# An attention and expert-routing kernel with its written order of steps replaced by another

## Chip, cores and metric

The kernel runs on one core of a Trainium2 chip. The metric is the device time of one execution in microseconds; lower is better. Three runs of the kernel before were timed.

## What is computed

The inputs are q, k and v of 8 batches, 8 heads, 576 positions and 64 channels in float32, 4608 token ids, and the weights of 8 experts. Attention without a score matrix (softmax over channels for q, over positions for k) gives 4608 rows of 512; each row then goes through the one expert that its token id selects.

```python
q_s = softmax(q, axis=-1)
k_s = softmax(k, axis=2)
kv  = einsum('bhsd,bhse->bhde', k_s, v)
x   = einsum('bhsd,bhde->bhse', q_s, kv)      # as 4608 rows of 512
...
expert_idx = token_ids * 2654435761 % 8
for e in range(8):
    h = maximum(x[expert_idx == e] @ w1[e], 0)    # 512 -> 1024
    out[expert_idx == e] = h @ w2[e]              # 1024 -> 512
```

## The kernel before

First an index part sorts the tokens by expert on the chip: each expert has 640 slots, five blocks of 128. Then the work is cut into named steps. `_Steps` collects them, and the loop over `ORDER` at line 974 runs them one after the other; each step appends its instructions to the engines that it uses, so the order of the names is the order of every engine's instructions and of the transfers on POOL's queue (manual scheduling; the framework adds the waits). The names, with e an expert, b a batch and i or r a part:

- `K3`, `V3`: loads of k and v of a batch (L784, L788; k of batches 0 to 2 is loaded by SP, v of 0 and 1 by POOL, ahead of all steps). `EKb` is the exponential of k on ACT (L355, L356), `MKb` a copy of ones into v (L361), `KVb` the product k'v on PE, 20 matmuls (L373), `SCb` its scaling on DVE (L382 to L388).
- `Ge_i`: gather of 128 rows of q for block i of an expert (L396; O stands for the overflow rows). `EQ` is their exponential on ACT (L406), `SM` and `ML` sums and scaling on DVE (L416, L422), `TP` transposes on PE (L432), `TC` the copy out (L895, L887).
- `PPe_..`, `PCe_..`: x = q'(kv) on PE (L443 for experts 0 and 1, L455 after) and the copy out (L925, L931). `XP`, `XC`, `SH`, `SD`, `SI`, `SE` do the same for tokens beyond an expert's 72 per batch (L465 to L483).
- `We1_i`, `We2_i`: half i of the weights w1 or w2 of expert e (L508), into two sets of buffers, for even and odd experts, so that the weights of expert 3 wait until expert 1's layer is done. `Ae_lo_i`: matmuls of the first layer (L523); `R`: its relu (L536 on ACT, L538 on DVE); `Be_i`: second layer for one block, 8 matmuls (L545); `C`: copy out (L954 ACT, L956 DVE); `S`: scatter to the output (L550).
- `CNT`, `OVA`, `OHA`, `FND`, `FDD`, `QS`, `ROP`, `ROD`: overflow tokens. `ANY`: all engines read a flag and branch around a general path that these inputs don't need (L835, L836).

Half i of w1 holds 256 of the 512 rows of the matrix. A first-layer group accumulates four chunks of 128 rows for each 128 columns, the first two from half 0:

```python
for i in range(len(f)):
    for dc in range(DC):
        nc.tensor.matmul(p, lhsT=w1r[:, dc, f[i] * 128:(f[i] + 1) * 128], rhs=X[:, dc, :], start=(dc == 0), stop=(dc == DC - 1))
```

A name in the set `SWAP` sends that step's copy to the other of the two engines ACT and DVE (`other`, L486). A number behind a name, as in `KV2*9`, repeats so many matmuls of a constant before the step's own (L345, L346), into the bank that the step then overwrites. Between a load and a later transfer there is one more bond: a transfer from POOL reuses the semaphore of the eighth before it and waits for it.

Of the kernel before, what the change touches and what calls it, by code (L numbers as in the profile page):

```python
# [689 lines left out]
ORDER = """  # L690
ZO0 CNT MK0 OVA G0_2 OHA FND G0_1 G0_0 EK1 V2 ZO1 MK1 EQ0_0 G0_3 EK0 EQ0_2 EQ0_1 K3 EK2 FDD ANY V3 KV1 G0_4 SM0a G1_1
ML0a TP0_1 EQ0_3 EK3 KV0 GO_0 SC1 EQ0_4 EQ1_1 MK2 MK3 TC0_1 QS GO_1 SM0b K4 TP0_0 ROP G1_2 TC0_0 TP0_2 EQO_0 EQO_1
G1_0 SC0 K5 ML0b SMOa KV2*9 EQ1_0 GO_2 ROD GO_3 KV3 MLOa TC0_2 TP0_3 EQ1_2 TC0_3 EQO_2 TPO_0 TCO_0 G1_3 V4 SC3 SC2
SM1a TP0_4 EQ1_3 TC0_4 SM1b TPO_1*7 EQO_3 EK5 XP0*4 TCO_1 XP1 PP0_03 ML1a EK4 V5 MK5 PC0_03 XC0 PP0_02*4 XC1 K6 TP1_0
TC1_0 V6 ML1b K7 MK4 PC0_02 V7 TP1_1 W01_1 SH3 SH1 TC1_1 PP0_00 PP0_01 W01_0 EK6 G2_0 SMOb KV5 PC0_01 TP1_2 SD1 SH2
PC0_00 MLOb TP1_3 MK6 TC1_2 PP1_02 KV4 TC1_3 SD2 G3_1 PP1_03 PC1_02 TPO_3 EK7 SC5 MK7 SH0 SC4 TCO_3 G2_1 PC1_03 KV6
G2_2 TPO_2 SC6 TCO_2 PP0_41 SD3 KV7 SD0 PC0_41 PP0_43 PP0_42 SC7 XP2 PC0_42 PP0_40 PC0_43 PC0_40 PP1_01 XP3 PC1_01
PP0_61 XC2 G3_0 PP0_62 G3_2 PC0_61 PP1_43 XC3 PC0_62 W11_1 PP1_40 PC1_43 SI1 PC1_40 SI3 PP1_42 PP1_00 SE1 G3_3 PC1_42
PC1_00 A0_0_2 SI0 EQ3_1 SE3 PP0_63 A0_0_0 W11_0 PP0_60 G2_3 R0_0_2 SE0 W02_1 SI2 PC0_63 PP1_41 EQ3_0 R0_0_0 W02_0 G5_2
EQ2_1 G4_4 SM3a A0_0_1 R0_0_1 PC0_60 SE2 A0_0_3 PC1_41 ML3a R0_0_3 A0_576_0 EQ2_2 A0_432_0 A0_432_1 TP3_1 OV1 EQ2_0  # L700
R0_432_0 A1_0_0 R0_432_1 A1_320_3 G2_4 SM2a TP3_0 R1_0_0 ML2a TC3_1 EQ3_3 TC3_0 A1_0_3 TP2_1 R1_320_3 R1_0_3 TC2_1
W12_0 EQ3_2 A1_0_2 SM3b TP2_2 TC2_2 R0_576_0 TP2_0 A1_320_2 W12_1 EQ2_3 G6_2 G4_1 R1_320_2 ML3b B0_0 G5_3 TC2_0 B0_4
EQ2_4 C0_0 PP2_02 SM2b PC2_02 TP3_2 ML2b B0_1 TP3_3 A1_320_1 TC3_2 W21_0 G4_2 OV2 TP2_3 TC3_3 R1_0_2 TC2_3 TP2_4
A1_320_0 C0_4 C0_1 G7_2 G5_0 PP2_32 W21_1 R1_320_0 PC2_32 G4_3 TC2_4 B0_2 PP2_31 C0_2 PP2_03 PC2_31 PC2_03 A1_0_1
PP2_01 R1_0_1 B0_3 EQ5_3 S0_2 PP2_00 W31_0 OV4 PC2_00 R1_320_1 PC2_01 C0_3 B1_0 G5_1 PP2_33 G4_0 EQ5_2 EQ5_0 G7_3
W31_1 G6_3 PP2_30 PC2_33 S0_0 EQ4_3 B1_4 PC2_30 PP2_62 A2_0_1 A2_0_2 SM5b S0_3 PP2_63 PC2_63 C1_4 W22_1 ML5b C1_0
R2_0_2 EQ5_1 SM5a EQ4_2 B1_2 C1_2 R2_0_1 S0_1 A2_0_0 TP5_2 B1_1 A3_0_2 EQ4_4 OV3 R2_0_0 A3_0_3 TC5_2 PC2_62 EQ4_1
W22_0 R3_0_2 PP2_61 SM4b C1_1 PC2_61 ML5a G7_0 A3_0_1 ML4b R3_0_1 PP2_60 B1_3 PC2_60 TP4_4 EQ7_2 G6_0 C1_3 G6_1
A3_320_3 EQ4_0 R3_0_3 TC4_4 A2_0_3 R3_320_3 A2_320_2 R2_0_3 A2_320_3 R2_320_2 A2_320_1 R2_320_3 TP5_0 SM4a OV5 ML4a
W32_0 TP4_2 EQ7_0 R2_320_1 A2_320_0 R2_320_0 TC5_0 G7_1 S1_4 A3_320_1 G6_4 R3_320_1 W41_1 TC4_2 EQ6_2 S1_1 B2_2 TP4_0  # L710
PP4_61 EQ6_4 PC4_61 EQ6_1 EQ6_0 B2_4 A3_320_2 TC4_0 A3_0_0 C2_4 W41_0 EQ7_1 R3_320_2 W32_1 PP4_31 EQ7_3 SM6a B2_3
R3_0_0 PC4_31 C2_2 ML6a PP4_01 PP4_60 B2_1 C2_3 PC4_60 PC4_01 PP4_30 EQ6_3 A3_320_0 PC4_30 S2_3 B2_0 A4_320_3 W51_0
S2_4 W42_1 C2_1 SM7b R3_320_0 C2_0 ML7b S1_2 R4_320_3 SM7a A4_320_1 PP4_00 ML7a B3_1 R4_320_1 B3_0 A4_320_0 PC4_00
TP7_2 SM6b R4_320_0 ML6b S0_4 W51_1 A4_320_2 TP6_2 C3_0 R4_320_2 B3_2 S2_1 TC6_2 A4_0_3 C3_1 B3_3 TC7_2 C3_2 B3_4
R4_0_3 S3_0 A4_0_2 R4_0_2 C3_3 S3_3 A5_320_3 R5_320_3 A5_0_3 R5_0_3 W42_0 S2_0 A4_0_1 A5_320_1 TP6_4 R4_0_1 A5_320_0
R5_320_1 S1_0 TC6_4 R5_320_0 S2_2 OV6 W52_1 S1_3 A4_0_0 R4_0_0 TP6_0 S3_2 TP7_0 W52_0 C3_4 W61_0 A5_0_1 PP6_60 PC6_60
B4_1 A5_320_2 B4_4 TC7_0 C4_1 TC6_0 R5_0_1 S4_1 R5_320_2 C4_4 A5_0_0 R5_0_0 PP6_01 B4_0 C4_0 A5_0_2 R5_0_2 B4_3 PP6_00
PC6_01 PP6_31 PC6_00 PC6_31 B5_1 C4_3 S3_1 S3_4 C5_1 PP6_30 PP6_61 B4_2 PC6_30 C4_2 PC6_61 A6_0_2 A6_0_1 R6_0_1 B5_2
A6_320_1 R6_0_2 B5_3 W71_0 A6_0_0 S4_3 C5_3 B5_4 W62_0 OV7 R6_320_1 C5_4 A6_0_3 R6_0_0 R6_0_3 A6_320_0 C5_2 S4_2 B5_0
A7_0_2 S5_1 R6_320_0 A6_320_3 B6_0 R7_0_2 R6_320_3 S5_3 A6_320_2 S4_4 A7_320_0 C6_0 R6_320_2 S5_2 A7_320_2 R7_320_2  # L720
W72_0 B6_2 C5_0 S5_0 R7_320_0 A7_0_3 R7_0_3 C6_2 B6_1 A7_0_1 B6_3 R7_0_1 C6_1 S5_4 A7_320_3 C6_3 R7_320_3 A7_0_0 B6_4
C6_4 R7_0_0 B7_0 A7_320_1 C7_0 B7_1 S4_0 C7_1 R7_320_1 B7_3 B7_2 S6_2 S6_3 S6_0 C7_3 S6_4 S7_0 C7_2 B7_4a S6_1 S7_1
S7_3 S7_2 C7_4a B7_4b C7_4b S7_4
""".split()


# [299 lines left out]
```

## Time and profile before

| | |
|---|---|
| median of 3 runs | 222.04 us (221.56 to 222.4) |
| the profiled execution | 222.7 us, span of the trace 220.9 us |
| PE busy | 187.5 us, 85% of the span |
| DVE, ACT, POOL busy | 133.6, 113.7, 120.2 us |
| moved by DMA | 50.67 MB in 12904 packets |

Busy time is summed over the span, and an engine can be busy off the path that sets the end; the queues of transfers have a row of their own. A line of a timeline gives the start, the duration and in brackets the idle time before it with what ended it. Ends of matmuls are modelled and overlap the next start, so a matmul's pace is read from the distance of starts.

### The profile page before, as it was taken

The page shows a single profiled execution, that of the slowest core. Times are in us where ns is not written, and L with a number is a line of the kernel's source. Part 1 is how long each engine was busy: PE and PEld are TensorE (multiplying, and loading weights), DVE is VectorE, ACT ScalarE, POOL GpSimd, SP SyncE. Part 2 cuts the span into 40 slices and gives each one's busy share as a digit, 9 for nine tenths or more (in the row PEclk, how much of TensorE's full clock was granted, in tenths as well). Part 3 has the DMA queues.
Part 4 walks back from the last instruction along what each step waited for, and adds up shares of the span by engine and source line. Part 5 has one row for each costly group of instructions (what it writes and reads, how often), then busy time and mean ns, then how long its engine had stood idle before and what let it go on. Part 6 is the DMA issues. An engine that isn't in the chain of part 4 may idle for free.

```text
span 220.9 us, 3984 instructions
## 1 busy us (share of the span) xinstructions
PE 187.5 (85%) x1534; PEld 122.2 (55%) x1534; DVE 133.6 (60%) x260; ACT 113.7 (51%) x183; POOL 120.2 (54%) x152
## 2 busy tenths in 40 slices
PE   3501098669899999999899999999999999999990
...
PEclk9999999999999999999999999999999999999998
DMA  6999999999999999999996969938999996751342
GB/s 203 327 329 287 330 391 384 240 314 305 240 326 254 271 251 309 227 234 206 261 223 164 205 144 158 213 104 153 277 237 237 207 167 225 136 179 47 136 175 98
DMA packets 12904, 50.67 MB, mean 229 GB/s; under 512 B 2522, under 2 KB 2522, under 8 KB 11344
## 3 DMA queue, kind: packets, MB, share of 16 engines
...
q1 hardware_dynamic: 576, 3.71, 4.4%
...
## 4 chain that ended last, share of the span: by engine, by line
PE 51%; DVE 13%; issue 11%; POOL 6%; DMA 4%; POOLq 1%; ACT 1%; ACTq 0%
PE ph L523 24%; PE po L545 19%; POOL out_dram L550 6%; DMA w1r<-in_moe_w_dram 4%; DVE kvr L388 3%; PE t L432 3%; DVE rq L416 3%; DVE qs L422 2%; PE px L455 2%; PE t L443 1%; PE t L373 1%; PE t L472 1%; DVE XT L925 1%; DVE rec L384 1%; DVE XTov L478 1%
## 5 line engine op out<-in xcount | busy, mean ns | idle before, releaser
L523 PE MATMUL ph<-XT,w1r 128*128 128x320 f16 (+2 forms) x512 | 75.3, 297 | 1.3 <-DMA w1r<-in_moe_w_dram 1.3
L545 PE MATMUL po<-w2r,hT 128*128 128x512 f16 (+2 forms) x328 | 74.5, 374 | 0.0
L536 ACT ACTIVATE hT<-ph 128x640 f16<-128x640 f32 (+3 forms) x59 | 41.6, 709 | 57.6 <-PE ph L523 50.7
L550 POOL DMA_INDIRECT out_dram<-ob,sidx x40 | 41.6, 1041 | 51.7 <-DVE ob L956 32.5
L523 PEld LDWEIGHTS <-w1r 128*128 128x128 f16 x544 | 49.1, 98 | 23.0 <-DMA w1r<-in_moe_w_dram 1.6
L396 POOL DMA_INDIRECT raw<-in_q_dram,gidx x36 | 44.0, 1223 | 19.9 <-issue 6.9
L545 PEld LDWEIGHTS <-hT 128*128 128x128 f16 x328 | 31.2, 98 | 31.0
L956 DVE TENSOR_SCALAR ob<-po 128x512 f32<-128x512 f32 x32 | 21.6, 682 | 43.3 <-PE po L545 35.7
L416 DVE TENSOR_REDUCE rq<-qs 128x16 f32<-128x1024 f16 (+1 forms) x18 | 23.9, 1329 | 3.9 <-ACT qs L406 3.8
L406 ACT ACTIVATE qs<-raw 128x512 f16<-128x512 f32 x36 | 21.8, 630 | 7.3 <-DMA raw<-in_q_dram,gidx 5.5
L422 DVE TENSOR_TENSOR qs<-qs,rq 128x1024 f16<-128x1024 f16 (+1 forms) x18 | 24.0, 1337 | 0.2
L895 DVE COPY qT<-t 128x512 f16<-128x512 f16 (+1 forms) x19 | 9.9, 528 | 13.5 <-PE t L432 12.8
L432 PE MATMUL t<-ident,qs 128*128 128x128 f16 x160 | 13.7, 222 | 2.2 <-DVE qs L422 1.7
L432 PEld LDWEIGHTS <-qs 128*128 128x128 f16 x160 | 11.1, 100 | 4.5 <-ACT qT L895 1.8
L508 POOL DMA_DIRECT2D w1r<-in_moe_w_dram x14 | 8.2, 586 | 9.2 <-PE ph L523 6.7
L373 PE MATMUL t<-v,w1r 128*128 128x129 f16 x64 | 7.0, 266 | 5.3 <-ACTq L836 5.3
L508 POOL DMA_DIRECT2D w2r<-in_moe_w_dram x14 | 8.3, 595 | 5.5 <-PE po L545 3.0
L954 ACT ACTIVATE ob<-po 128x512 f32<-128x512 f32 (+2 forms) x9 | 4.9, 552 | 11.7 <-PE po L545 11.6
L925 ACT CAST XT<-t 128x288 f16<-128x288 f32 (+2 forms) x17 | 6.5, 400 | 7.8 <-PE t L443 7.7
L925 DVE CAST XT<-t 128x288 f16<-128x288 f32 (+2 forms) x15 | 6.5, 447 | 5.2 <-PE t L443 5.1
L931 ACT CAST XT<-px 128x864 f16<-128x864 f32 (+1 forms) x7 | 5.7, 810 | 6.7 <-PE px L455 6.7
L256 PE MATMUL po<-Z,AO 128*128 128x8 f16 x18 | 0.6, 175 | 9.9 <-DVE AO L244 9.9
(128 smaller groups left out, 197.5 us busy)
## 6 DMA issues: line engine op xcount, KB each, us to landing
...
```

The costliest lines, as they stand in the source:

```text
L396: nc.gpsimd.indirect_dma_start(out=raw[:, :], out_offset=None, in_=self.q[:, :], in_offset=bass.IndirectOffsetOnAxis(ap=idx[:, i:i + 1], a ...
L406: self.nc.scalar.activation(q16[:, i].rearrange("p h d -> p (h d)"), raws[i][:, :], ACT.Exp)
L416: nc.vector.reduce_sum(rv, qv, axis=AX.X)
L422: nc.vector.tensor_tensor(out=qf, in0=qf, in1=rv.rearrange("p i h -> p (i h)").unsqueeze(2) .to_broadcast([128, (hi - lo) * H_, DH_]), op= ...
L432: nc.tensor.transpose(pv[:, r, 128 * j:128 * j + 128], rq16[1][:, i + j, 2 * r:2 * r + 2, :] .rearrange("p h d -> p (h d)"), self.ident[:])
L508: self.nc.gpsimd.dma_start(w[what - 1][:, f], src[e, :, f])
L523: nc.tensor.matmul(p, lhsT=w1r[:, dc, f[i] * 128:(f[i] + 1) * 128], rhs=X[:, dc, :], start=(dc == 0), stop=(dc == DC - 1))
L536: self.nc.scalar.activation(to, fro, ACT.Relu)
L545: nc.tensor.matmul(po[:, 0:d.stop - d.start], lhsT=hT[:, fc, blk * 128:(blk + 1) * 128], rhs=w2r[:, fc, d], start=(fc == 0), stop=(fc == F ...
L550: sc = self.nc.gpsimd.indirect_dma_start(out=self.out[:, :], out_offset=bass.IndirectOffsetOnAxis(ap=self.ix.sidx[:, e, blk:blk + 1], axis=0),
L925: (A if other(f"PC{e}_{lo}{r}", r % 2 == 0) else V)(X[:, es, r, lo * CELL:hi * CELL], px[e, r, lo])
L956: nc.vector.tensor_scalar(out=obs[e, blk][:, d], in0=po[e, blk, x][:, 0:d.stop - d.start], scalar1=1.0 / SX, scalar2=None, op0=ALU.mult)
```

## The change

The tables `SWAP` and `ORDER` are replaced; no function is touched. The set of steps is the same, with the same transfers and buffers. In the new order W31_1 and W31_0, the two halves of expert 3's w1, follow each other on POOL's queue. The repeats go from 24 (KV2*9, TPO_1*7, XP0*4, PP0_02*4) to 30 (TP0_1*16, TP0_0*10, KV5*4). Cut to one line of each table:

```diff
 SWAP = set("""
-TC1_0 SD1 PC0_00 SD2 TCO_3 PC0_43 PC0_62 R0_0_3 TC2_0 C0_0 C0_2 R1_320_1 PC2_01 C0_3 PC2_30 PC2_63 PC2_61
...
+TCO_1 TCO_0 TC0_4 PC0_01 PC0_03 SD0 PC0_42 PC1_03 XC2 PC0_62 R0_0_2 C1_3 PC2_31 C1_4 C1_2 R3_0_0 TC4_2 C2_2
...
 ORDER = """
-ZO0 CNT MK0 OVA G0_2 OHA FND G0_1 G0_0 EK1 V2 ZO1 MK1 EQ0_0 G0_3 EK0 EQ0_2 EQ0_1 K3 EK2 FDD ANY V3 KV1 G0_4 SM0a G1_1
...
-PP2_01 R1_0_1 B0_3 EQ5_3 S0_2 PP2_00 W31_0 OV4 PC2_00 R1_320_1 PC2_01 C0_3 B1_0 G5_1 PP2_33 G4_0 EQ5_2 EQ5_0 G7_3
-W31_1 G6_3 PP2_30 PC2_33 S0_0 EQ4_3 B1_4 PC2_30 PP2_62 A2_0_1 A2_0_2 SM5b S0_3 PP2_63 PC2_63 C1_4 W22_1 ML5b C1_0
...
+G0_0 ZO0 G0_1 CNT G1_0 OVA OHA FND FDD ANY EK1 MK1 MK0 EK0 EQ0_1 KV1 K3 EQ0_0 ZO1 SC1 G0_2 EQ0_2 G1_1 V2 EK3
...
+PC2_01 EQ5_1 B0_1 G6_0 C0_0 C0_1 EQ5_2 PP2_00 PP2_03 PC2_00 B1_0 C1_0 W31_1 B1_3 C1_3 PP2_32 W31_0 SM5a B0_3
...
```

POOL's queue around expert 3's weights, before (w1r_1573 is expert 2's buffer, w1r_1679 expert 3's, w2r_1574 expert 2's second layer; raw are gathers, out_0_dram scatters):

```order
L508 DMA w1r_1573<-in_moe_w1_dram 128x2048
L396 DMA raw_1622<-in_q_dram,gidx_271 128x512
L550 DMA out_0_dram<-ob_1640,sidx_782 4608x512
L508 DMA w1r_1679<-in_moe_w1_dram 128x2048
L396 DMA raw_1697<-in_q_dram,gidx_271 128x512
L396 DMA raw_1705<-in_q_dram,gidx_271 128x512
L396 DMA raw_1711<-in_q_dram,gidx_271 128x512
L508 DMA w1r_1679<-in_moe_w1_dram 128x2048
L396 DMA raw_1716<-in_q_dram,gidx_271 128x512
L550 DMA out_0_dram<-ob_1527,sidx_782 4608x512
L550 DMA out_0_dram<-ob_1686,sidx_782 4608x512
L508 DMA w2r_1574<-in_moe_w2_dram 128x2048
```

And now (w1r_1615 is expert 2's buffer, w1r_1691 expert 3's, w2r_1616 expert 2's second layer):

```order
L508 DMA w1r_1615<-in_moe_w1_dram 128x2048
L550 DMA out_0_dram<-ob_1613,sidx_885 4608x512
L396 DMA raw_1662<-in_q_dram,gidx_271 128x512
L508 DMA w1r_1691<-in_moe_w1_dram 128x2048 x2
L550 DMA out_0_dram<-ob_1601,sidx_885 4608x512
L508 DMA w2r_1616<-in_moe_w2_dram 128x2048 x2
```

The three gathers between the halves are gone, one scatter and one gather stand ahead of both, and expert 2's second layer follows after one scatter.

ACT's queue at the start, before: the ones of v, the exponentials of k (kraw) and of q (raw), and the read of the flag with which the step ANY begins.

```order
L361 COPY v16_0_140<-two_95 128x20x2
L355 ACTIVATE w1r_299<-kraw1_138 128x2048
L356 ACTIVATE kt1_98<-kraw0_136 64x512
L361 COPY v16_1_142<-two_95 128x16x2
L406 ACTIVATE qs0_109<-raw_358 128x512
L355 ACTIVATE w1r_299<-kraw0_136 128x2048
L356 ACTIVATE kt0_97<-kraw0_136 64x512
L406 ACTIVATE qs0_109<-raw_329 128x512
L406 ACTIVATE qs0_109<-raw_354 128x512
L355 ACTIVATE w2r_300<-kraw2_144 128x2048
L356 ACTIVATE kt2_99<-kraw2_144 64x512
L835 TENSOR_LOAD flag_296
```

And now, first the flag, and from the end of the general path on, the first exponentials:

```order
L336 COPY kvr7_108<-zero_126 128x512
L837 TENSOR_LOAD flag_296
...
L355 ACTIVATE w1r_299<-kraw1_138 128x2048
L356 ACTIVATE kt1_98<-kraw0_136 64x512
L361 COPY v16_1_142<-two_95 128x16x2
L361 COPY v16_0_140<-two_95 128x20x2
L355 ACTIVATE w1r_299<-kraw0_136 128x2048
L356 ACTIVATE kt0_97<-kraw0_136 64x512
L406 ACTIVATE qs0_109<-raw_307 128x512
L406 ACTIVATE qs0_109<-raw_301 128x512
L406 ACTIVATE qs0_109<-raw_605 128x512
L355 ACTIVATE w2r_300<-kraw3_595 128x2048
```

The branch stands ahead of all exponentials now, the ones of v of batch 0 (v16_0) behind those of batch 1, and the k of batch 3 is taken before that of batch 2.

## Rows read from the trace of the kernel before

**Rows 1.** The page's part 2: the span in 40 slices, busy share in tenths.

```profile
PE   3501098669899999999899999999999999999990
...
PEclk9999999999999999999999999999999999999998
DMA  6999999999999999999996969938999996751342
```

**Rows 2.** Waits of PE over the whole span: total us, times, longest us.

```profile
PE ph L523 <- DMA w1r<-in_moe_w_dram: 1.3, 1, 1.3
```

**Rows 3.** Timeline of PE: start us, us, instructions, [idle before <-releaser].

```profile
62.33 1.63 PE L523 MATMUL ph<-XT,w1r 128*128 128x432 f16 x8
...
104.00 0.43 PE L523 MATMUL ph<-XT,w1r 128*128 128x320 f16 x2
105.70 2.08 PE L523 MATMUL ph<-XT,w1r 128*128 128x320 f16 x14 [1.26 <-DMA w1r<-in_moe_w_dram]
...
208.78 7.09 PE L545 MATMUL po<-w2r,hT 128*128 128x512 f16 x40
```

**Rows 4.** Timeline of POOL, which issues the transfers: same columns.

```profile
17.45 0.60 POOL L784 DMA_DIRECT2D kraw<-in_k_dram  x1
...
57.06 0.99 POOL L396 DMA_INDIRECT raw<-in_q_dram,gidx  x1 [1.47 <-DMA v<-in_v_dram]
...
62.41 1.02 POOL L396 DMA_INDIRECT raw<-in_q_dram,gidx  x1 [1.32 <-DMA w1r<-in_moe_w_dram]
...
91.30 0.62 POOL L508 DMA_DIRECT2D w1r<-in_moe_w_dram  x1
...
95.19 1.00 POOL L396 DMA_INDIRECT raw<-in_q_dram,gidx  x1 [0.61 <-ACT qs L406]
96.19 0.60 POOL L508 DMA_DIRECT2D w1r<-in_moe_w_dram  x1
...
215.13 0.98 POOL L550 DMA_INDIRECT out_dram<-ob,sidx  x1 [0.74 <-issue]
216.46 0.98 POOL L550 DMA_INDIRECT out_dram<-ob,sidx  x1 [0.35 <-issue]
```

**Rows 5.** The chain that ended last, around 96 us: start us, us, what.

```profile
96.19 9.46 DMA w1r<-in_moe_w_dram
```

**Rows 6.** Timeline of ACT, first steps and the last of the keys.

```profile
13.49 1.91 ACT L355 ACTIVATE w1r<-kraw 128x2048 f16<-128x2048 f32 x1
...
18.20 0.22 ACT L361 COPY v<-two 128x32 f16<-128x32 f16 x1 [2.15 <-DMA v<-in_v_dram]
20.66 0.63 ACT L406 ACTIVATE qs<-raw 128x512 f16<-128x512 f32 x1 [2.24 <-DMA raw<-in_q_dram,gidx]
...
54.35 1.91 ACT L355 ACTIVATE w2r<-kraw 128x2048 f16<-128x2048 f32 x1 [0.33 <-DMA kraw<-in_k_dram]
...
56.94 0.22 ACT L361 COPY v<-two 128x32 f16<-128x32 f16 x1
```

**Rows 7.** Lines 835 and 836, the branch on the routing flag, on SP.

```profile
L835 SPq TENSOR_LOAD <-flag x1: 457/457/457, 14.8 to 14.8; - x1
...
L836 SPq EVENT_SEMAPHORE  x8: 17/17/17, 16.2 to 18.7; - x8
```

**Rows 8.** Timeline of PE again: one form early and late, and the repeats.

```profile
27.56 0.64 PE L373 MATMUL t<-v,w1r 128*128 128x129 f16 x4
...
28.10 0.64 PE L373 MATMUL t<-v,w1r 128*128 128x129 f16 x4
...
33.14 2.17 PE L346 MATMUL t<-rowi,ident 128*128 128x512 f16 x9
...
39.82 0.61 PE L432 MATMUL t<-ident,qs 128*128 128x128 f16 x8 [1.66 <-DVE qs L422]
...
50.30 0.39 PE L373 MATMUL t<-v,w1r 128*128 128x129 f16 x4
...
50.58 0.39 PE L373 MATMUL t<-v,w1r 128*128 128x129 f16 x4
```

More of the change, by code (lines that the diff above doesn't have):

```diff
@@ L685 @@
 SWAP = set("""
-TC1_0 SD1 PC0_00 SD2 TCO_3 PC0_43 PC0_62 R0_0_3 TC2_0 C0_0 C0_2 R1_320_1 PC2_01 C0_3 PC2_30 PC2_63 PC2_61
-R2_320_1 C2_4 PC4_31 C2_0 C4_2 C6_4 R7_0_0 C7_4a C7_4b
+TCO_1 TCO_0 TC0_4 PC0_01 PC0_03 SD0 PC0_42 PC1_03 XC2 PC0_62 R0_0_2 C1_3 PC2_31 C1_4 C1_2 R3_0_0 TC4_2 C2_2
+TC4_4 R4_0_0 C5_4 R6_0_2 C7_4a C7_4b
 """.split())
 ORDER = """
-ZO0 CNT MK0 OVA G0_2 OHA FND G0_1 G0_0 EK1 V2 ZO1 MK1 EQ0_0 G0_3 EK0 EQ0_2 EQ0_1 K3 EK2 FDD ANY V3 KV1 G0_4 SM0a G1_1
-ML0a TP0_1 EQ0_3 EK3 KV0 GO_0 SC1 EQ0_4 EQ1_1 MK2 MK3 TC0_1 QS GO_1 SM0b K4 TP0_0 ROP G1_2 TC0_0 TP0_2 EQO_0 EQO_1
@@ L693 @@
[L693 to L702, printed above, removed]
```

52 lines of the change are left out of this document (33 added, 19 removed).

## Prediction

> **What bounds the kernel now.** I read the page's busy rows first. From the eleventh of the 40 slices TensorE shows 9 or more tenths to the last slice; before that it is mostly waiting, while the DMA row shows 9 from the second slice to the twentieth [rows 1]. So there are two stages, a front that feeds and a long stage that multiplies, and a time saved counts in the second stage only if TensorE stops idling there, or if that stage starts sooner.
>
> Where does the second stage start, and does it idle? The timeline of TensorE gives both. The first layer of expert 0 starts at 62.33 us and the last second-layer matmuls end at 208.78 + 7.09 = 215.87 us [rows 3]. In these 153.54 us the list of waits has one wait only, 1.26 us before a weight half of a first layer [rows 2, 3]. It stands after two matmuls of a step, and a first-layer step runs through half 0 of its weights for two matmuls before it needs half 1: the step is A3_0_2, the weights are expert 3's w1. So the stage is 152.28 us of matmuls and 1.26 us of idling, and
>
> end = start of A0 + 152.28 + idling + what follows the last matmul.
>
> What sets the start? POOL's timeline shows when a transfer has landed, since a transfer reuses the semaphore of the eighth before it. The last v load is down at 57.06 us and the second half of expert 0's w1 at 62.41 us [rows 4]. A0 starts at 62.33, as these weights land. ScalarE waits 0.33 us for the last k load at 54.35 us and marks the last v at 56.94 us, so the attention chain has almost no slack either [rows 6]. The front is bound by the DMA, with ScalarE close behind.
>
> And the stall? Half 0 of expert 3's w1 is issued at 91.30 us, half 1 only at 96.19 us: three query gathers stand between, the last of which waits 0.61 us for ScalarE to free its buffer [rows 4]. The chain that ended last runs through that second half: 9.46 us from issue to landing, at 105.65 us [rows 5].
>
> **The change, part by part.**
>
> *Expert 3's two halves side by side.* In the new order W31_1 and W31_0 follow each other with nothing between. Their gate is the same as before: expert 1's first layer must be through with the buffer, and the scatter and the gather ahead of them on POOL must be issued. If the first goes out at 91.30 as before, the second follows 0.62 us later, at 91.9. With the 9.46 us of the old second half it lands at 101.4. Expert 3's first step now also comes later on TensorE: one more second-layer block and one more first-layer group, 16 matmuls, stand ahead of it, and at 2.08/14 = 0.149 us each [rows 3] that is at least 2.4 us. So it comes near 107 us and its weights have about 5 us to spare. The stall goes: **-1.26 us**. Bounds: -1.26, and 0 if the halves are late for another reason. I take the lower end, because 5 us is more than all that moved. What is late next? Expert 2's second layer, whose halves are issued right behind expert 3's, and they are needed seven first-layer groups after A3 begins, 7 x 8 x 0.149 = 8.3 us; I see no wait there.
>
> *The start of A0.* The loads ahead of expert 0's w1 are the same transfers as before, all k, all v, the gathers of experts 0 and 1 and of the overflow rows, in another order. The DMA row is full all along, so the floor is no gain. It could be up to 0.4 us earlier, since W01_0 now goes first and two of the eight matmuls of A0's first row need only that half: 1.63 x 2/8 = 0.4 [rows 3]. What could make it later is the branch on the routing flag (the step ANY). ScalarE used to take it after the key exponentials EK1, EK0 and EK2; now it stands ahead of EK1. The flag is read at 14.8 us and the branch's semaphores are done from 16.2 us on [rows 7], so EK1, at 13.49 before, starts near 16.2, 2.7 us later. K3's load, now fourth on the queue, waits for EK1 to free its buffer: 16.2 + 1.91 = 18.1 us against 17.45 [rows 4, 6]. The queue is not empty then, as the gathers issued ahead of it are down only at 20.66 us [rows 6]. ScalarE itself waited 2.15 + 2.24 = 4.39 us for transfers before it got to EK0 [rows 6], which can swallow the 2.7. Later the exponentials for expert 0's fourth block stand behind two more gathers and both v loads, so some waits come back. Bounds for the start: -0.4, and +2.7 if nothing is absorbed. I take **+0.5**, near the lower end, because the row with 4.39 us of waits is the nearest to it.
>
> *Work after the start.* Steps moved across A0 cancel: before, SI0, SI2, PP0_63, PP0_60 and PP1_41 were still owed then, now SI1, SI0, PP1_43 and PP1_42. Both are 4 matmuls of 512 and 8 of 72 columns: 0.
>
> *The repeated matmuls* that keep TensorE busy in the front go from 24 to 30. At 2.17/9 = 0.24 us [rows 8] that is 1.4 us more, all ahead of A0 in the stage where TensorE waits; it is hidden while KV5, which carries four of them, is not the last thing ScalarE waits for. If that cover is gone, 4 x 0.24 = 1.0 us come on top.
>
> *Copies between VectorE and ScalarE* (the names swapped in the set): 24 names instead of 26. In the long stage both engines are far from full, so 0; in the front it is part of the +0.5.
>
> *The end.* The last scatter starts at 216.46, 0.59 us after the last matmul, because POOL is inside the scatter before it until 215.13 + 0.98 = 216.11 [rows 4]. The new order puts S7_3 earlier against the last block, so **-0.15**; bounds -0.35 (the last wait) and 0.
>
> Sum: -1.26 + 0.5 - 0.15 = -0.91 us. The profiled execution took 222.7 us, so 221.8; that execution lay 0.66 above the median of the three runs, 222.04, which makes **221.1 us** in the median.
>
> [...] The old repeats begin at 33.14 us with KV2 [rows 8] and go on with TPO_1, XP0 and PP0_02; the new ones come with TP0_1 and TP0_0, ahead of that, and then only with KV5, so that the stretch from KV2 to KV4, which waits much for VectorE, has none.
> [...]
>
> **The rivals.**
>
> *The front is bound by the DMA alone.* Then the start comes 0 to 0.4 us earlier, 0.2 in the middle: -1.26 - 0.2 - 0.15 = -1.6, **220.4 us**. For it: the full DMA row. Against it: ScalarE waits only 0.33 us for the last k load.
>
> *The stall stays or moves* to another weight half, as every order of 32 loads has a tightest one. Then +0.5 - 0.15 = +0.35, **222.4 us**. For it: the DMA row is full or nearly so to the middle of the span [rows 1]. Against it: the 5 us to spare.
>
> [...]
>
> **How the numbers follow.** A measurement of this kernel can tell about 0.5%, 1.1 us, from no change, so "faster" is below 220.9 and "slower" above 223.2. Chances: the forecast 0.48, whose spread of some 0.8 us puts 0.20 below 220.9 and 0.28 above; the DMA alone 0.19, 0.18 of it faster and 0.01 same; the stall elsewhere 0.13, same; the low level 0.20, of which 0.17 slower and 0.03 same. Faster 0.38, same 0.45, slower 0.17. The range reaches from the DMA rival less its 0.4 us of half-order and 0.2 us of end, 219.8, to the low-level rival, 223.3; outside lie half of that rival and some 0.08 below.
>
> **What would show it.** Right: no wait of TensorE for w1 after A0; the two halves of expert 3's w1 issued under 1.5 us apart and down before 104 us; A0 between 62.0 and 63.5 us; 152.3 us of matmuls from there to the end. Wrong: A0 later than 64 us, with ScalarE's last key exponential past 55.5 us; matmuls of KV4 or KV5 at 0.108 us; a new wait of TensorE for a weight half or for a copy after A0.

## The result and the profile after

The changed kernel took 224.96 us in the median of 4 runs (223.46 to 225.0), the kernel before 222.07 us on the same chip (221.56 to 222.4, 4 runs). The ratio is 1.0121 with a 95% interval of 1.0097 to 1.0146: slower by 2.7 us by this ratio, where 221.1 us and a range of 219.8 to 223.3 us were predicted. The execution profiled took 225.0 us, its span is 223.2 us (before 222.7 and 220.9). In this table the two profiled spans are taken apart:

| | before | after | difference |
|---|---|---|---|
| start of A0 | 62.33 | 66.35 | +4.02 |
| TensorE's wait for expert 3's w1 half | 1.26 | none | -1.26 |
| matmuls from A0 to the last | 152.28 | 152.04 | -0.24 |
| end of the last matmul to the end of the span | 5.03 | 4.81 | -0.22 |
| span | 220.9 | 223.2 | +2.30 |

So TensorE's wait, which the two halves side by side were to remove, is gone in this execution, -1.26 us as forecast, and the front gave back three times as much. The rows that answer to [rows 3], from the timeline of PE after (A0, expert 3's first step A3_0_3, and the last second-layer matmuls, which end at 209.57 + 8.82 = 218.39):

```profile
66.35 1.63 PE L523 MATMUL ph<-XT,w1r 128*128 128x432 f16 x8
...
110.57 1.25 PE L523 MATMUL ph<-XT,w1r 128*128 128x320 f16 x8
...
209.57 8.82 PE L545 MATMUL po<-w2r,hT 128*128 128x512 f16 x48
```

Expert 3's first step runs through its 8 matmuls in one row, without the break that stood at 105.70 before. It begins 44.22 us after A0, before 41.67. For [rows 4], the timeline of POOL after:

```profile
14.45 1.00 POOL L396 DMA_INDIRECT raw<-in_q_dram,gidx  x1 [0.31 <-issue]
18.14 0.58 POOL L786 DMA_DIRECT2D kraw<-in_k_dram  x1 [2.70 <-DVE at L235]
19.03 2.96 POOL L396 DMA_INDIRECT raw<-in_q_dram,gidx  x1 [0.31 <-issue]
...
46.30 0.53 POOL L790 DMA_DIRECT2D v<-in_v_dram  x1 [5.01 <-PE t L373]
...
63.13 1.00 POOL L396 DMA_INDIRECT raw<-in_q_dram,gidx  x1 [1.48 <-DMA w1r<-in_moe_w_dram]
...
94.66 1.17 POOL L508 DMA_DIRECT2D w1r<-in_moe_w_dram  x2
...
218.99 0.98 POOL L550 DMA_INDIRECT out_dram<-ob,sidx  x1 [0.30 <-ACT ob L956]
```

Both halves of expert 3 go out together at 94.66. But at 18.14 the load K3 is issued after 2.70 us in which POOL issues nothing, and V6, at 38.47 before, waits for KV2 until 46.30. Behind K3's late issue the DMA share falls to 0.79 and 0.83 for 4 us, where it is 1.04 and 1.03 before. In the table of stretches, the last three columns are TensorE's granted clock, the DMA engines' busy share and GB/s; first before, then after:

```profile
20.00:22.00 2.00, 0.65 (x18) 0.56 (x18) 1.89 (x3) 1.34 (x2) 1.99 (x1) 1.00 1.04 215
22.00:24.00 2.00, 0.00 (x0) 0.00 (x0) 0.86 (x8) 2.00 (x3) 1.41 (x2) 1.00 1.03 378
```

```profile
20.00:22.00 2.00, 0.65 (x18) 0.56 (x18) 1.24 (x3) 2.00 (x4) 1.99 (x1) 1.00 0.79 289
22.00:24.00 2.00, 0.32 (x4) 0.35 (x5) 1.12 (x7) 0.25 (x1) 1.70 (x3) 1.00 0.83 303
```

From 39 to 45.6 us, while V6 waits, the share is 1.02 again (row under e5).

For [rows 6], the timeline of ACT after:

```profile
15.94 1.91 ACT L355 ACTIVATE w1r<-kraw 128x2048 f16<-128x2048 f32 x1 [9.56 <-ACTq L838]
...
34.55 0.63 ACT L406 ACTIVATE qs<-raw 128x512 f16<-128x512 f32 x1 [5.41 <-DMA raw<-in_q_dram,gidx]
...
58.49 1.92 ACT L355 ACTIVATE w2r<-kraw 128x2048 f16<-128x2048 f32 x1
```

EK1 starts when the branch on the flag is done, 15.94, and ends at 17.85; K3, whose buffer it frees, is issued 0.29 us later. (The row of POOL names DVE at L235, which came last there; K3 needs nothing of it, since it goes out at 17.45 before, ahead of that instruction at 17.72.) ScalarE then waits 5.41 us for the gather of G0_3, which stands behind K3, two other gathers and two v loads, and the last key exponential EK7 starts at 58.49 instead of 54.35. The timeline of PE serves the repeats and the granted clock: the transposes of TP0_1 behind their 16 repeats, the wait in which the clock falls (1.00 from 36 to 39 us, 0.50 behind), KV2 and the first row of KV4; then the clock row of the page's part 2.

```profile
32.58 0.38 PE L432 MATMUL t<-ident,qs 128*128 128x128 f16 x4 [0.55 <-DVE qs L422]
...
39.61 0.61 PE L432 MATMUL t<-ident,qs 128*128 128x128 f16 x4 [2.07 <-DVE qs L422]
...
43.67 0.64 PE L373 MATMUL t<-v,w2r 128*128 128x129 f16 x4
...
44.21 0.64 PE L373 MATMUL t<-v,w2r 128*128 128x129 f16 x4
...
50.69 0.64 PE L373 MATMUL t<-v,w1r 128*128 128x129 f16 x4
```

```profile
PEclk9999999587999999999999999999999999999999
```

What the late start is made of stands in the chain of waits that ended last (start us, us, what), first of the change, then of the kernel before:

```profile
29.38 10.64 DMA rawo<-in_q_dram,oidx
...
43.87 2.14 PE t L373 x20
...
50.89 2.04 PE t L373 x20
52.93 0.86 PE t L346 x4
53.79 1.14 PE t L373 x20
```

```profile
31.85 1.14 DVE rq L416
...
34.80 1.22 DVE qs L422
...
46.30 0.86 PE t L346 x4
```

The chain of the change goes through the gather of the overflow rows, GO_0. It is issued at 29.38, before at 23.63, and ScalarE has its rows only at 40.02. KV2 and KV4 follow in the chain: KV2 runs at (44.21 - 43.67)/5 = 0.108 us per matmul and takes 2.14 us, KV4 2.04, and KV5, at (53.91 - 53.63)/5 = 0.056 us per matmul, 1.14. The granted clock is 0.50 from 39 to 45.6 us and 0.51 from 49.2 to 52.4, and 1.00 from 53 to 66: a stretch near 0.5, in which KV's matmuls come every 0.108 us, is called the low level here. The 1.9 us that KV2 and KV4 take longer than KV5 are the low level's part of this chain. The weights are not in it: the gather at 63.13 shows the first half of expert 0's w1 landed 3 us ahead of A0. The chain of the kernel before goes through VectorE's work from 29 to 60 us, but for 2 us of TensorE's around 46.30. So there were three suspects for the 4 us: the flag ahead of EK1 with K3 behind it, the low level, and the order on ScalarE and VectorE.

### The profile page after: what moved, and what is told of

Same layout as the page of the kernel before. It is cut to its first block, busy times and chain, and to the rows that moved or that the text cites. A ratio compares the mean times of both kernels' runs of the same rounds, so it can differ in the third digit from the quotient of the medians.

```text
span 223.2 us, 3990 instructions
## 1 busy us (share of the span) xinstructions
PE 192.2 (86%) x1540; PEld 125.9 (56%) x1540; DVE 135.4 (61%) x262; ACT 112.3 (50%) x181; POOL 117.8 (53%) x152
## 4 chain that ended last, share of the span: by engine, by line
PE 40%; issue 24%; POOL 11%; DMA 5%; ACT 4%; DVE 4%; POOLq 1%; ACTq 0%; DVEq 0%
PE ph L523 16%; PE po L545 14%; POOL out_dram L550 10%; DMA rawo<-in_q_dram,oidx 5%; PE t L373 4%; PE t L432 2%; PE t L443 1%; POOL w2r L508 1%; DVE kvr L388 1%; ACT qT L897 1%; PE t L472 1%; PE px L455 1%; ACT w2r L355 1%; DVE rq L416 1%; ACT qs L406 1%
## 5 line engine op out<-in xcount | busy, mean ns | idle before, releaser
L523 PE MATMUL ph<-XT,w1r 128*128 128x320 f16 (+2 forms) x512 | 73.8, 297 | 0.0
L396 POOL DMA_INDIRECT raw<-in_q_dram,gidx x36 | 39.8, 1104 | 20.9 <-issue 5.8
L958 DVE TENSOR_SCALAR ob<-po 128x512 f32<-128x512 f32 x34 | 23.3, 687 | 39.4 <-PE po L545 39.2
L432 PE MATMUL t<-ident,qs 128*128 128x128 f16 x160 | 14.4, 230 | 6.0 <-DVE qs L422 2.6
L897 DVE COPY qT<-t 128x512 f16<-128x512 f16 (+1 forms) x18 | 9.0, 511 | 10.7 <-PE t L432 10.5
L355 ACT ACTIVATE w1r<-kraw 128x2048 f16<-128x2048 f32 x4 | 7.6, 1909 | 9.6 <-ACTq L838 9.6
L933 DVE CAST XT<-px 128x864 f16<-128x864 f32 (+1 forms) x6 | 5.7, 953 | 7.8 <-PE px L455 7.8
L927 ACT CAST XT<-t 128x288 f16<-128x288 f32 (+2 forms) x18 | 7.4, 421 | 5.3 <-PE t L443 5.1
L373 PE MATMUL t<-v,w1r 128*128 128x129 f16 x64 | 7.9, 288 | 1.9 <-DVEq L838 1.9
L956 ACT ACTIVATE ob<-po 128x512 f32<-128x512 f32 (+2 forms) x7 | 3.7, 537 | 10.6 <-PE po L545 10.6
```

The costliest lines, as they stand in the source:

```text
L373: nc.tensor.matmul(pkv[:, r // 2, r % 2, 0:129], lhsT=k16t[:, f] if last else k16[:, c, f], rhs=v16s[e][:, c * NPAIR + r, 0:129] if last e ...
L396: nc.gpsimd.indirect_dma_start(out=raw[:, :], out_offset=None, in_=self.q[:, :], in_offset=bass.IndirectOffsetOnAxis(ap=idx[:, i:i + 1], a ...
L432: nc.tensor.transpose(pv[:, r, 128 * j:128 * j + 128], rq16[1][:, i + j, 2 * r:2 * r + 2, :] .rearrange("p h d -> p (h d)"), self.ident[:])
L958: nc.vector.tensor_scalar(out=obs[e, blk][:, d], in0=po[e, blk, x][:, 0:d.stop - d.start], scalar1=1.0 / SX, scalar2=None, op0=ALU.mult)
```

## The experiments

Each edit is a change of the written order of one of the two kernels, with all steps kept. Each run and the kernel before were timed on the same chip, but not all runs on one chip, so runs are compared by their ratios to the kernel before.

**e1: the halves alone.** In the kernel before, one name moved:

```diff
-W31_0 OV4 PC2_00 R1_320_1 PC2_01 C0_3 B1_0 G5_1 PP2_33 G4_0 EQ5_2 EQ5_0 G7_3 W31_1
+W31_0 W31_1 OV4 PC2_00 R1_320_1 PC2_01 C0_3 B1_0 G5_1 PP2_33 G4_0 EQ5_2 EQ5_0 G7_3
```

> The kernel before, with expert 3's second w1 half issued right behind its first and nothing else moved. If the new place of that half is what removed TensorE's 1.26 us of idling, the start of A0 stays at 62.3 us, no wait for w1r is left behind it, the span is 219.6 us (220.9 - 1.26) and the median near 220.8 us. If the stall only moves (to another weight half or to the gathers now issued later), the span is 220.5 to 221 us and the median near 222.

222.1 us (10 runs) against 221.94 (15 runs); ratio 1.0015, 0.9994 to 1.0035. In its profile the wait is gone, A0 starts at 62.70 and the span is 220.0, 0.9 under that of before. But in the median nothing is won. Either most executions have no such wait, or a shorter one, or they lose the time elsewhere; the profiled ones alone do not tell which.

**e8: the kernel before, profiled again.**

> The kernel before, unchanged, profiled once more on this chip. If the 1.26 us wait for expert 3's second w1 half belongs to every execution: the wait is 1.1 to 1.4 us again. If it varies with the arrival of transfers: under 0.8 us or none, in an execution whose span is under 220.5 us.

222.47 us, span 220.7, A0 at 62.66. The wait is there, with 0.77 us in place of 1.26:

```profile
105.46 2.08 PE L523 MATMUL ph<-XT,w1r 128*128 128x320 f16 x14 [0.77 <-DMA w1r<-in_moe_w_dram]
```

The span was not the short one that the expectation tied to a small wait. What varies is seen in the list of DMA issues around 96 us, where the last figure is the time from issue to landing: 9.46 us in the first execution of before [rows 5], here 9.0, and in e7 (below), whose queue is the same there, 7.8 and no wait. First e8, then e7:

```profile
w1r<-in_moe_w_dram POOLq DMA_DIRECT2D x1, 512.0 KB, 9.0
```

```profile
w1r<-in_moe_w_dram POOLq DMA_DIRECT2D x1, 512.0 KB, 7.8
```

**e2: the old front, the new order behind it.** Up to A0 the order of before, then the remaining steps of the change in their order; what the new front holds beyond the old one is put between:

```diff
 PP1_42 PP1_00 SE1 G3_3 PC1_42 PC1_00
+G2_4 PP0_63 W11_0 PP1_41 PC0_63 PC1_41 SE3 G4_2 SI2 PP0_60 EQ2_4 SE2
+A0_0_0 R0_0_0 EQ3_3 SI0 A0_0_3 G4_4 EQ3_2 PC0_60 R0_0_3
...
```

> Steps up to the first layer of expert 0 in the written order of before (with their choice of copy engine and their repeats), the remaining steps in the order of the change. If all of the loss lies in the front: A0 at 62.3 us, no wait for w1r after it, 152.0 us of matmuls, span 219.6 us, median near 220.8 us. If part of the loss lies behind the start of A0 (copies, scatters), span above 220.5 us with A0 at 62.3 us.

228.21 us, ratio 1.0296 (1.0245 to 1.0346), A0 at 63.88. It doesn't tell the front of the change from its rest, since the joint makes a wait of its own: EQ2_4 follows its gather at once and stands ahead of the first relu on ScalarE (timeline of ACT), and TensorE waits for that relu (timeline of PE).

```profile
69.26 0.63 ACT L406 ACTIVATE qs<-raw 128x512 f16<-128x512 f32 x1 [6.06 <-DMA raw<-in_q_dram,gidx]
69.80 0.87 ACT L536 ACTIVATE hT<-ph 128x864 f16<-128x864 f32 x1
```

```profile
70.72 1.62 PE L523 MATMUL ph<-XT,w1r 128*128 128x432 f16 x8 [3.33 <-ACT hT L536]
```

In this run one gather with its use right behind it cost TensorE these 3.33 us.

**e3: the flag back.** In the changed kernel:

```diff
-FDD ANY EK1 MK1 MK0 EK0 EQ0_1 KV1 K3 EQ0_0
+FDD EK1 MK1 MK0 EK0 EQ0_1 K3 ANY KV1 EQ0_0
```

> The changed kernel, with the branch on the routing flag put back behind EK1, EK0, EQ0_1 and the issue of K3 (and KV1 behind it), nothing else. If the flag's delay of EK1 (15.94 us instead of 13.49) and with it of K3's load makes the late start: EK1 back near 13.5 us, A0 1.5 to 2.5 us earlier than 66.35, median 222.5 to 223.5 us. If the delay is swallowed by ScalarE's later waits for transfers (5.41 us before EQ0_3), A0 stays within 0.5 us of 66.35 and the median near 225.

223.75 us (6 runs), ratio 1.0062 (1.0023 to 1.0101); EK1 at 12.81, K3 issued at 15.46 right behind the gathers, ScalarE's wait before EQ0_3 2.56 us instead of 5.41, A0 at 63.68, 2.67 earlier. So the flag matters, but by which way? ScalarE's first exponentials of q came no earlier than in the change, at 21.05 against 21.12, which points to the transfers. By the ratios 1.3 us come back, with intervals that just overlap.

**e6: K3 behind two gathers, the flag kept first.** In the changed kernel:

```diff
-KV1 K3 EQ0_0 ZO1 SC1 G0_2 EQ0_2 G1_1 V2
+KV1 EQ0_0 ZO1 SC1 G0_2 EQ0_2 G1_1 K3 V2
```

> The changed kernel with the flag's branch kept first, but the load K3 (whose buffer comes free only when EK1 is done) issued behind the gathers G0_2 and G1_1 instead of ahead of them. If the flag costs its time through POOL's queue, with K3 blocking what is issued behind it while the DMA queues run dry at 20 to 24 us: POOL's 2.70 us of idling ahead of K3 goes, the DMA share is 1.0 from 20 to 24 us, the gather for EQ0_3 lands at 31 to 32.5 us instead of 34.55, A0 is 1.5 to 2.5 us earlier, median 222.5 to 223.7 us. If it costs it through ScalarE, whose exponential EK1 starts at 15.94: A0 stays within 0.5 us of 66.35, median near 225.

222.46 us (10 runs), ratio 1.0024 (1.0004 to 1.0044) where the change has 1.0121: one load moved by two places on POOL's queue takes back 2.2 us, and the intervals lie apart. EK1 still starts at 15.95. POOL's timeline has no idle time ahead of K3 any more. Of the 2.70 us, 1.24 remain ahead of the gather at 16.69, where the branch stands in POOL's order; the rest was the wait for EK1. The DMA engines are full from 20 us (same columns as above):

```profile
16.69 0.99 POOL L396 DMA_INDIRECT raw<-in_q_dram,gidx  x1 [1.24 <-DVE m L227]
17.99 1.00 POOL L396 DMA_INDIRECT raw<-in_q_dram,gidx  x1 [0.31 <-issue]
18.99 0.59 POOL L784 DMA_DIRECT2D kraw<-in_k_dram  x1
```

```profile
20.00:22.00 2.00, 0.65 (x18) 0.56 (x18) 1.25 (x2) 2.00 (x4) 1.70 (x3) 1.00 1.04 361
22.00:24.00 2.00, 0.37 (x4) 0.40 (x5) 1.11 (x7) 0.97 (x2) 1.39 (x3) 1.00 1.03 378
```

The gather of EQ0_3 is there at 31.72, and GO_0 is issued at 25.59 instead of 29.38. One thing moves along with it: KV2 now runs at 0.056 us per matmul, the granted clock is 0.51 from 48 to 50 us, 0.64 from 50 to 52 and 1.00 in the rest from 36 to 56, so up to 1.0 of the 2.2 us can be the clock's (20 matmuls, 2.14 us in the change and 1.15 here). The execution profiled, 223.93 us, is the longest of the ten, and its A0 at 65.29 is only 1.06 earlier; why, its chain of waits shows (start us, us, what):

```profile
30.14 5.61 PE t L346 x16
35.75 0.22 PE t L432 x4
35.97 2.16 PE t L346 x10
```

The repeats stand in the chain: TP0_1, whose input VectorE has scaled at 32.3, waits behind its 16 until 35.75, and TP0_0 behind 10 more.

**e7: the flag first in the old order.** In the kernel before:

```diff
-FND G0_1 G0_0 EK1 V2 ZO1 MK1 EQ0_0 G0_3 EK0 EQ0_2 EQ0_1 K3 EK2 FDD ANY V3
+FND G0_1 G0_0 FDD ANY EK1 V2 ZO1 MK1 EQ0_0 G0_3 EK0 EQ0_2 EQ0_1 K3 EK2 V3
```

> The kernel before, with only the branch on the routing flag (and the vector step FDD) put ahead of EK1. EK1 starts near 15.9 us. By the theory of the blocked queue K3 stands behind V2 and G0_3 here, POOL loses under 1 us, ScalarE swallows the rest in its 4.39 us of waits for transfers: A0 at 62.3 to 63.2 us, median 222 to 222.8. If the delay of EK1 itself runs down ScalarE's chain: A0 at 64.3 to 65 us, median 224 to 224.8.

221.32 us (10 runs, 221.14 to 221.77) against 222.17 (19 runs, 221.32 to 222.97); ratio 0.9967, 0.9951 to 0.9982. EK1 is as late as in the change, and the kernel is faster than before. V2 and G0_3 go out ahead of K3 while EK1 runs:

```profile
16.42 0.58 POOL L788 DMA_DIRECT2D v<-in_v_dram  x1 [0.96 <-DVE mine L220]
17.31 1.03 POOL L396 DMA_INDIRECT raw<-in_q_dram,gidx  x1 [0.31 <-issue]
18.34 0.59 POOL L784 DMA_DIRECT2D kraw<-in_k_dram  x1
```

**e9: K3 at the head in the old order.** The order of e7 with K3 moved:

```diff
-FDD ANY EK1 V2 ZO1 MK1 EQ0_0 G0_3 EK0 EQ0_2 EQ0_1 K3 EK2
+FDD ANY EK1 K3 V2 ZO1 MK1 EQ0_0 G0_3 EK0 EQ0_2 EQ0_1 EK2
```

> The kernel before with the flag's branch ahead of EK1, as in the run named e7 (221.32 us), and in addition the load K3 issued first behind the branch, ahead of V2 and G0_3. By the theory of the blocked queue this puts the loss of the change into the old order: POOL idles about 2.7 us ahead of K3 (issue at 18.1 us), the DMA share falls under 0.9 from 20 to 24 us, and the kernel loses 1.5 to 2.5 us against e7: A0 at 64 to 65.2 us, median 222.8 to 223.8 us. If K3's place does not matter by itself (the change lost its time to its orders on ScalarE or VectorE): A0 within 0.4 us of e7's 62.70, median 221.2 to 221.7.

223.01 us (10 runs), ratio 1.002 (0.9996 to 1.0044): 1.2 us more than e7 by the ratios (1.69 by the medians, on two chips), and the intervals lie apart. POOL idles as in the change, GO_0 is issued at 25.42 instead of 23.68, A0 is at 65.25; the DMA share in 20 to 22 us is 0.91 and 1.07 in the next 2 us, so the queue hardly ran dry, against 0.79 and 0.83 in the change. The price is that of the order: what stands behind K3 goes out later.

```profile
18.01 0.58 POOL L784 DMA_DIRECT2D kraw<-in_k_dram  x1 [2.71 <-DVE at L235]
18.58 0.59 POOL L788 DMA_DIRECT2D v<-in_v_dram  x1
```

The execution profiled, 224.22 us, is the longest of the ten, and its granted clock is 0.66 over 40 to 50 us. But the loss does not need the low level: the four executions of e9 with a mean granted clock of 1.0 took 222.49 to 223.17 us, and none of the ten of e7 more than 221.77. With e6 this is the same cause taken out of one order and put into the other: 2.2 and 1.2 us.

**e4 and e12: the repeats exchanged.** e4 is the changed kernel with the repeats of before, e12 the kernel before with those of the change:

```diff
-TP0_1*16 ... TP0_0*10 ... KV5*4
+KV2*9 ... TPO_1*7 ... XP0*4 ... PP0_02*4
```

> The changed kernel, with the repeated matmuls taken from TP0_1, TP0_0 and KV5 and put where they stood before (9 with KV2, 7 with TPO_1, 4 with XP0, 4 with PP0_02), all else as in the change. If the low level of TensorE's clock from 39 to 52 us makes the late start: matmuls of KV2 and KV4 at 0.056 us, POOL's issue of V6 some 1 to 2 us before 46.3, A0 at 63.5 to 65 us, median 222 to 223.7 us. If the feeding of the front alone sets the start, the low level goes and A0 stays within 0.5 us of 66.35, median near 225.

> The kernel before with the repeats of the change: 16 with TP0_1, 10 with TP0_0 and 4 with KV5, none with KV2, TPO_1, XP0 and PP0_02. If the place of the repeats is a cause of its own: low granted clock somewhere from 39 to 53 us, KV2 or KV4 at 0.108 us, A0 0.5 to 1.5 us later, median 222.7 to 223.7. If they are covered in this order: A0 within 0.3 us of 62.5, median 221.8 to 222.4.

Both lose: e4 227.29 us, ratio 1.0214 (1.0161 to 1.0267); e12 227.41 us, ratio 1.0177 (1.0103 to 1.0251). In e4 no repeats stand ahead of KV2, the granted clock is 0.62 in 30 to 40 us and 0.70 in 40 to 50, and KV2's 9 repeats take 3.70 us in the timeline, where 2.17 was the price before [rows 8]; 3.50 of them stand in its chain of waits:

```profile
42.96 3.50 PE t L346 x9
```

In e12 the 16 repeats stand in front of TP0_1, which ran at 29.18 in the kernel before, and ScalarE waits for the transposes behind the repeats (timelines of PE, where the first of the 16 lies ahead of this row, and ACT); the low level comes later (granted clock 0.63 in 44 to 46 us, 0.50 from 46 to 54):

```profile
29.76 3.95 PE L346 MATMUL t<-rowi,ident 128*128 128x512 f16 x15
33.55 0.39 PE L432 MATMUL t<-ident,qs 128*128 128x128 f16 x4
```

```profile
37.49 0.58 ACT L895 COPY qT<-t 128x512 f16<-128x512 f16 x1 [2.93 <-PE t L432]
```

**e5: more repeats.** The changed kernel with 22 more, in the gaps that TensorE has from 37.6 to 49.2 us:

```diff
-TP0_3 ... TP0_2 ... TPO_1 ... TPO_0 ... XP0
+TP0_3*8 ... TP0_2*6 ... TPO_1*2 ... TPO_0*4 ... XP0*2
```

> The changed kernel with its 30 repeats kept and 22 more put where TensorE idles between 37.6 and 49.2 us: 8 with TP0_3, 6 with TP0_2, 2 with TPO_1, 4 with TPO_0, 2 with XP0. If the low level of TensorE's clock is a cause: granted clock 1.00 from 39 to 53 us, KV2 and KV4 at 0.056 us, V6 issued 1 to 2 us before 46.3, A0 between 64.3 and 65.5 us, median 223 to 224 us. If the clock only follows from the late feeding and is covered by other waits: the clock rises, A0 stays within 0.4 us of 66.35, median near 225. If the repeats stand in the way of ready work: A0 later than 66.8.

225.12 us, ratio 1.0169 (1.0107 to 1.023): no gain in the median. Its four executions took 223.69, 224.81, 225.42 and 227.23 us at mean granted clocks of 1.0, 0.996, 0.987 and 0.981. The first is the one profiled, and the shortest: the clock stays at 1.00 and A0 comes at 65.02, 1.33 earlier than in the change. Stretches of the change, then of e5 (PEclk is the third last figure):

```profile
39.00:45.60 6.60, 3.99 (x34) 3.61 (x35) 5.79 (x13) 5.79 (x9) 1.62 (x3) 0.50 1.02 249
49.20:52.40 3.20, 3.20 (x32) 3.20 (x33) 3.07 (x5) 2.98 (x8) 2.10 (x2) 0.51 1.02 281
```

```profile
39.00:45.60 6.60, 4.20 (x45) 2.89 (x44) 5.73 (x14) 5.80 (x9) 1.91 (x5) 1.00 1.02 247
49.20:52.40 3.20, 3.20 (x51) 2.73 (x49) 3.03 (x7) 2.94 (x8) 1.52 (x2) 1.00 1.03 253
```

So this one execution without the low level starts A0 1.33 us earlier. In the other three, whose mean clock is lower, that is gone; they have no profile that shows where.

**e11, e13, e14, e15: what is left in e6.** One edit on top of e6 each, but for e14 (on e13) and e15 (on e14):

```diff
 e11
-V3 ... G0_3 G0_4
+G0_3 G0_4 V3
 e13
-TP0_1*16 ... TP0_0*10
+TP0_1*6 ... TP0_0
 e14
-TPO_1 ... TPO_0
+TPO_1*5 ... TPO_0*4
 e15
-SC1 ... SM0a QS
+SM0a QS SC1
```

> The run named e6 (222.46 us) with the load V3 issued behind the gathers G0_3 and G0_4 as well, so that the two v loads, which move some 205 GB/s from 24 to 28 us, no longer stand together ahead of the gathers. If the order of these loads is what is left of the loss: ScalarE's wait of 2.48 us ahead of EQ0_3 shrinks to under 1.2 us, A0 0.5 to 1.2 us earlier than e6's 65.29, median 221.3 to 222.0. If the rest lies in ScalarE's and VectorE's order: the wait only moves behind (rawo), A0 within 0.3 us, median 222.2 to 222.7.

> The run named e6 (K3 behind the gathers, 222.46 us) with 6 repeats instead of 16 with TP0_1 and none instead of 10 with TP0_0; the 4 with KV5 stay. In e6's profile TP0_1 stands behind its 16 repeats until 35.58 us, while its input is ready at 32.4, and TP0_0 behind 10 more. If the repeats have become the bound there, once the loads come earlier: TP0_1 at 32.5 to 33.5 us, A0 1 to 2.5 us earlier than e6's 65.29, median 220.8 to 221.8 us. If they are needed to hold the clock: granted clock 0.5 in more of 30 to 53 us than e6's 48 to 51, median 222.5 to 225. If the work behind waits for loads anyway: median 222.2 to 222.7.

> The run named e13 with 5 repeats with TPO_1 and 4 with TPO_0 besides, where TensorE idled 1.55 and 1.26 us in e6. If the clock's fall at 48 us costs KV4 its 20 x 0.052 = 1.0 us and these repeats prevent it: KV4 at 0.056 us, 0.5 to 1 us faster than e13. If the clock does not fall in e13 or the repeats stand in the way: no gain, or up to 1 us slower than e13.

> The run named e14 (222.25 us) with VectorE's step SC1 behind SM0a and QS instead of ahead of SM0a. In e14 VectorE idles until 25.99 us for SC1's matmuls (KV1), then works without a gap from 27.4 to 45 us, and the chain runs through it. SM0a's input is there at about 25.5 us. If VectorE's late start is the rest of the loss: SM0a at 25.5 to 26 us, VectorE's row 0.5 to 1.4 us earlier, A0 at 62.8 to 63.7 us instead of 64.17, median 221.2 to 221.8. If ScalarE or the transfers are as late on their own: A0 within 0.3 us of 64.17, median 222.0 to 222.5.

e11 takes 223.49 us, ratio 1.006 (1.0024 to 1.0096), a loss against e6: the waits for the gathers go, and ScalarE waits 3.21 us at 32.92 for V3 instead (the execution profiled, 222.89 us, has A0 at 63.61, but the ten reach 225.2). e13: 222.43, ratio 1.0008 (0.9988 to 1.0028); TP0_1 now runs at 32.45, but the granted clock is 0.50 to 0.51 from 38 to 50 us, and KV2 and KV4 run at 0.108 (the execution profiled, 223.56 us, is the longest of the ten). e14: 222.25, ratio 1.0021 (1.0005 to 1.0036); the granted clock is 0.67 in 44 to 46 us and 1.00 from 46 to 56, KV4 runs at 0.056. e15: 222.22, ratio 1.0003 (0.9973 to 1.0032); VectorE's first sum starts at 24.40 instead of 27.36, and the chain then runs through a transfer, the overflow gather. These three can't be told from e6: in their profiles, where one chain is cut, another of nearly the same length sets the start (A0 at 64.81, 64.17 and 64.26 us, in e6 at 65.29). e13 also says something of the low level: the executions of the change had mean granted clocks of 0.974 to 0.984 and took 223.46 to 225.0 us; the seven of e13 within the same clocks took 221.78 to 222.63.

**e10: e7 with the halves.** The move of e1 on top of e7.

> The run named e7 with expert 3's second w1 half issued right behind the first as well. If what hid the gain of the halves was only the spread of the front's end, e7's narrower spread (221.14 to 221.77 us) shows it: 0.3 to 0.8 us less than 221.32. If e7 has no such wait left in most executions (its profile shows none): median 221.2 to 221.5 us, no difference.

221.65 us (10 runs, 221.24 to 223.8), ratio 0.9983 (0.9946 to 1.002): no gain over e7. e7 is the fastest version of all, 0.3% under before and 1.5% under the change. e7's profile shows A0 at 62.70, no wait for expert 3's weights, and a span of 219.5. Why its executions lie so close together was not tried.

## Why the prediction was wrong, step by step

**The halves, -1.26.** The mechanism was right: no wait of TensorE for w1 behind A0, halves issued back to back (94.66) and down some 8.6 us later; expert 3's first step came 2.55 us later behind A0, where "at least 2.4" was forecast, and its weights had some 7 us to spare, not 5. The size failed. It was read from one execution, and the text itself said that this execution lay 0.66 us above the median of the runs; the wait that was to be removed may be part of what made it long. The landing took 9.46, 9.0 and 7.8 us in three executions of the same queue, the wait 1.26, 0.77 and none, and in the median its removal is worth nothing that can be told (e1: ratio 0.9994 to 1.0035; e10 against e7 neither). Taking off the wait and then the 0.66 as well counts the gain twice if the median execution has less of the wait; that it does was not shown.

**The start of A0, +0.5.** This is the step that failed: +4.02 in the profiled execution. Its parts came out as worked: EK1 "starts near 16.2" (15.94), K3's load "16.2 + 1.91 = 18.1 us against 17.45" (18.14). The sentence that went wrong is the next: "The queue is not empty then, as the gathers issued ahead of it are down only at 20.66 us." It priced K3's own delay, 0.65 us, and not that of what stands behind K3. In the old order with the flag first, e7, V2 and G0_3 are issued while EK1 runs; in the new one POOL issues nothing for 2.70 us, and the DMA engines fell to 0.79 and 0.83 of their time from 20 to 24 us. The full DMA row of [rows 1] was read as a property of the front, so that a late issue would be made up; it held only while enough was issued (0.79 and 0.83 from 20 to 24 us in the change, 1.04 and 1.03 in e6). The two shares are worth 0.21 x 2 + 0.17 x 2 = 0.8 us of transfers; the rest is that single transfers came later, of which GO_0, 3.8 us later than in e6, stands in the chain. The upper bound of +2.7 was for the same reason no bound: it was ScalarE's delay alone. e6 and e9 price the blocked queue at 2.2 and 1.2 us, of which a part in e6 can be the clock's, and e7 shows that ScalarE's delay alone costs nothing in the old order, as the absorbing 4.39 us of waits suggested.

The reading under this term was too simple as well. "The front is bound by the DMA, with ScalarE close behind" rests on the full DMA row and on the weights' landing near A0; the chain of the kernel before goes through VectorE, which the prediction does not weigh. And TensorE's row of [rows 1] shows 9, 8, 6, 6, 9 in slices six to ten, so it was not "mostly waiting" there; nothing of the sum hangs on that.

**Work after the start, 0.** Right: 152.04 against 152.28 us.

**The repeats, 0 while covered.** Half right. The 26 with TP0_1 and TP0_0 are covered in the change as it stands: none stands in the chain, and TensorE still waits 0.55 us for VectorE behind the first 16. They were covered by the lateness of everything else. The four with KV5 are not: 0.86 us of them stand in the chain, as the stated 1.0 us for a lost cover said, but four of PP0_02 stood in the chain before, with 0.86 us too. In e6's profile 7.8 us of repeats stand in the chain, though taking 20 of the 26 away gained nothing in the median (e13); in e12 they cost the old order 1.8%. What the 26 cost once they are not covered was not worked out.

**The copies, 0.** Not tried alone.

**The end, -0.15.** The last scatter starts 0.60 us behind the last matmul (218.99), before 0.59: 0. The 0.22 us at the end come from behind that scatter's start.

**The rivals.** TensorE's drop to the low level was given 223.3 us at a chance of 0.20, and its sign came true: KV4 at 0.108, A0 at 66.35, later than 64 us, EK7 at 58.49, past 55.5. But KV5 was not slow (0.056), and the low level is not shown to be the main part. It takes 1.9 us of the chain in the change. Yet with K3 moved e13 is no slower than the kernel before at the mean clock of the change, though it has 20 repeats less as well; e9 loses at a mean granted clock of 1.0 too; and e5 without the low level starts A0 1.3 us earlier in one execution and saves nothing in the median. No run shows the term behind the 223.3 us, a start made later by the low level alone; it was the author's estimate, and the runs show in its place the 1.9 us of the chain in the change and the 1.33 us of e5. The granted clock of the change fell from 1.00 to 0.50 at 39.0 us, in the wait of 2.07 us ahead of the row at 39.61; in the kernel before it reads 1.00 through the wait of 1.66 us at 39.82 [rows 8]. Which waits bring it down was not shown. The mean granted clock varies between executions of one kernel: three of e5 took 223.69, 224.81 and 225.42 us, 0.8% from first to last, at mean clocks of 1.0, 0.996 and 0.987. How much of that is the clock is not shown; in e6 the longest and the shortest execution, 223.93 and 222.0 us, have 0.992 and 0.99. That the DMA alone binds the front was wrong, as was the idea that the wait would move to another weight half: behind A0 there is none.

What stays open: how the 2.2 us of e6 divide between the queue and the clock, how the last 0.5 us of e6 against the kernel before divide among ScalarE's order, VectorE's and the clock, and why e7 is faster than the kernel before at all, where e1 without the wait is not.
